# Loading the weights of experts 0 and 1 ahead of the routing, and none for empty slots

## The chip, the cores and the metric

The kernel runs on one core of a Trainium2 chip. The metric is the device time of one execution in microseconds; the time before is the median of three runs. The core has five engines that run side by side, each through its own queue of instructions in order: TensorE (PE; matmuls, with its weight loads listed as PEld), VectorE (DVE), ScalarE (ACT), GpSimd (POOL) and SyncE (SP, which here only issues transfers). Transfers between main memory and the core's own memory run on 16 DMA engines that all queues share.

## The reference

Two layers follow each other: windowed attention, and a mixture of experts in which every token goes to exactly one expert.

```python
batch, n_heads, seq, head_dim = (8, 8, 576, 64)          # q, k, v
# heads 0-3 see the last 32 positions, heads 4-7 every 4th of the last 128
scores = np.where(masks, scale * q @ k.T, -1e9)
attn = exp(scores - max) / (sum + 1e-9)
x = (attn @ v)  ->  (B*S, H*D) = (4608, 512)             # bridge

N, D, E, F = (4608, 512, 8, 1024)                        # experts
logits = x @ w_gate
expert_idx = np.argmax(logits, axis=1)
gate_w = softmax(logits)[token, expert_idx]
for e in range(E):
    h = np.maximum(x_sorted[lo:hi] @ w1[e], 0.0)         # tokens of expert e
    y_sorted[lo:hi] = h @ w2[e]
return gate_w[:, None] * y
```

The experts' weights are 8 x 4 MB in float32: w1 is 512 x 1024 and w2 is 1024 x 512 for each expert, 2 MB each.

## The kernel before

Attention goes through 32 units, four for each of the eight sequences. When a sequence is done, its tokens are routed and their rows are scattered into a table in main memory, the bucket, with one region for each expert. An expert layer is computed in *slots* of 128 tokens of one expert. There are 43 slots, since 4608 tokens and eight part-filled tiles may need that many; slots at the end may stay empty. Which expert a slot gets is only known on the chip, when enough sequences have been routed. Seven stages do this: the first (after sequence 1) settles slots 0 and 1, the next slots 2 to 5, and so on; the last, after sequence 7, settles slots 24 to 42. Slots are computed between pieces of attention as soon as they are settled, and the remaining ones after attention has ended.

Attention, unit by unit, with its loads on the SyncE queue. Each `yield` is one round, at which other work may be put between:

```python
for i in range(len(units) + LAG + 1):
    if LAG <= i < len(units) + LAG:
        eTs = weights(evs.pop(i - LAG))         # transposes of the softmax, 9 on TensorE
        yield 1.1, None
    if i < len(units):
        evs[i], dens[i] = front(qT["q"], qT["k"], units[i][1])   # scores, masks, 9 exps on ScalarE
    if 0 < i <= len(units):
        norm(evs[i - 1], dens.pop(i - 1))       # den, rec on VectorE; product on GpSimd
    yield 1.1, None
    if i > LAG:
        row_part(...)                           # transposes xrow, gate logits
        yield 0.9, b2 if (ty2, hl2) == (1, 1) else None
    if i + 1 < len(units):
        for n in "qk":
            qT[n] = turn(b2, ty2, hl2, n)       # transposes "turned"
            yield 1.0, None
        if hl2 == 1 and b2 + 1 < B:
            load_qk(b2 + 1, ty2)
    if LAG <= i < len(units) + LAG:
        for part in range(2):
            summed(eTs, b2, xT, ty2, hl2, part) # xo = softmax times v
            if part == 1 and hl2 == 1 and b2 + 1 < B:
                load_v(b2 + 1, ty2)
            yield 0.75, None
```

The tables of a stage are small VectorE operations on one partition. Their end, where it is decided whether a slot's weights differ from those two slots earlier (the weights have two buffers, for even and odd slots):

```python
exs = cpool.tile([1, NSLOT], F32, name="exs")
...
ex = exs[:, j0:j1]
nc.vector.tensor_tensor(out=ge, in0=sel, in1=experts(const("eidx", 1)), op=OP.mult)
nc.vector.tensor_reduce(out=ex, in_=ge, axis=AX, op=OP.add)     # expert of each slot
... # base: where the slot's rows begin in the bucket
new = table("new", K)
if j0 == 0:
    nc.vector.memset(new[:, 0:2], 1.0)
lo = max(j0, 2)
if lo < j1:
    nc.vector.tensor_tensor(
        out=new[:, lo - j0 : K], in0=exs[:, lo:j1], in1=exs[:, lo - 2 : j1 - 2],
        op=OP.not_equal,
    )
```

The fetches of a slot, on SyncE: its rows x, and its weights under a condition. A slot's x and w1 are fetched once the slot two before has used its w1, its w2 once that slot has used its w2. A slot without tokens carries expert 7 in the list of experts.

```python
def fetch_w(j, dst, src):
    _, n, exi, _, newi = where[j]
    rv = nc.sync.value_load(exi[:, n : n + 1], min_val=0, max_val=E - 1)
    kw = {}
    if j >= 2:
        kw["cond"] = nc.sync.value_load(newi[:, n : n + 1], min_val=0, max_val=1) > 0
    nc.sync.dma_start(
        dst[j % 2], src[ds(rv, 1)].rearrange("o (c l) f -> l (o c) f", l=128), **kw
    )

wanted = []
for j in range(NSLOT):
    wanted += [(j, "x", 0, j - 1), (j, "w1", 0, j - 1), (j, "w2", 1, j - 1)]
```

A slot's work, cut: transposes of x (`xt`, copied out by VectorE), 16 matmuls for each half of `ph` (each matmul here shows as two records), the ReLU, 8 for `py`, the scaling by the gate on ScalarE, and a scatter of the finished rows by GpSimd. From slot 36 (SURE) on each slot stands in an `If`, which is left out when the slot is empty.

```python
for j in range(NSLOT):
    if j >= SURE:
        guards.enter_context(tc.If(live[0] > j))
    ...
    xt = across(j)                               # across(j + 1) in the first half of ph
    for fg in range(2):
        ... nc.tensor.matmul(ph[:, fi], lhsT=w1[:, c, ...], rhs=xt[:, c], ...)
        if fg == 1:
            done[0] = j + 1; fetch()
    for f in range(8):
        nc.tensor.matmul(py, lhsT=h[:, f], rhs=w2[:, f], start=f == 0, stop=f == 7)
    nc.scalar.activation(y, py, AF.Copy, scale=x[:, DM : DM + 1])
    late.append(scatter)
    done[1] = j + 1; fetch()
```

How slots are put among the attention rounds: a clock in model microseconds, counted while the program is built. A stage's slots may begin `BEHIND` after its tables are done, and are spread over the time until the next stage.

```python
ATT, BEHIND = 32.0, 12.0

def run_routing():
    ...
    ahead = STAGES[n + 1][0] - b if j1 < NSLOT else 1
    ready.append((clock["all"] + BEHIND, j1, ATT * ahead + 6.0))

for cost, ended in attention():
    clock["all"] += cost
    clock["owed"] += cost * clock["rate"] / 2 + 1e-6
    run_slots()
    ...
```

The order that the engines see is made when the program is built: a scheduler may move instructions of one engine against each other where their data allow it. On SyncE it gives the transfers eight semaphores in turn.

Of the kernel before, what the change touches and what calls it, by code (L numbers as in the profile page):

```python
# [10 lines left out]
F32 = mybir.dt.float32  # L11
I32 = mybir.dt.int32
AF = mybir.ActivationFunctionType
OP = mybir.AluOpType
# [6 lines left out]
N, DM, E, F = B * S, H * DH, 8, 1024  # L21
# [9 lines left out]
NSLOT = (N + E * 127) // 128  # L31
# [63 lines left out]
def kernel(  # L95
# [10 lines left out]
    nc = tc.nc  # L106
# [22 lines left out]
    nc.vector.memset(used, 0.0)  # L129
    avail = cpool.tile([128, E1], F32, name="avail")  # L130
    nc.vector.memset(avail[:, E:E1], 4.0 * NSLOT)
    exs = cpool.tile([1, NSLOT], F32, name="exs")

    def const(name, rows=128):
        a, w = at[name]
# [225 lines left out]
    def attention():  # L361


        units = [(b, ty, hl) for b in range(B) for ty in range(2) for hl in range(2)]
        for ty in range(2):
            load_qk(0, ty)
            load_v(0, ty)
        qT = {n: turn(0, 0, 0, n) for n in "qk"}
        evs, dens, xT = {}, {}, None
        for i in range(len(units) + LAG + 1):  # L370
            if LAG <= i < len(units) + LAG:
                eTs = weights(evs.pop(i - LAG))
                yield 1.1, None
            if i < len(units):
                evs[i], dens[i] = front(qT["q"], qT["k"], units[i][1])
            if 0 < i <= len(units):
                norm(evs[i - 1], dens.pop(i - 1))
            yield 1.1, None
            if i > LAG:
                b2, ty2, hl2 = units[i - LAG - 1]  # L380
                row_part(b2, 2 * ty2 + hl2, xT)
                yield 0.9, b2 if (ty2, hl2) == (1, 1) else None
            if i + 1 < len(units):
                b2, ty2, hl2 = units[i + 1]
                qT = {}
                for n in "qk":
                    qT[n] = turn(b2, ty2, hl2, n)
# [4 lines that stand above are left out]
                b2, ty2, hl2 = units[i - LAG]  # L392
                xT = pool.tile([128, S], F32, tag="xT", name="xT", bufs=3)
                for part in range(2):
                    summed(eTs, b2, xT, ty2, hl2, part)
# [3 lines that stand above are left out]
# [125 lines left out]
    def tables(s):  # L524
# [21 lines left out]
        if last:  # L546
# [22 lines left out]
            out=upto,  # L569
# [46 lines left out]
        nc.vector.tensor_tensor(out=ge, in0=slots(place), in1=experts(begin), op=OP.is_ge)  # L616
        nc.vector.tensor_tensor(out=sel, in0=sel, in1=ge, op=OP.mult)
        yield
        ex = exs[:, j0:j1]
        nc.vector.tensor_tensor(out=ge, in0=sel, in1=experts(const("eidx", 1)), op=OP.mult)  # L620
        nc.vector.tensor_reduce(out=ex, in_=ge, axis=AX, op=OP.add)
        first, base = table("first", E1), table("base", K)
# [23 lines left out]
                out=us[:, 0:E], in0=us[:, 0:E], in1=took[:, 0:E], op=OP.add  # L646
            )
        new = table("new", K)
        if j0 == 0:
            nc.vector.memset(new[:, 0:2], 1.0)  # L650
        lo = max(j0, 2)
        if lo < j1:
            nc.vector.tensor_tensor(
                out=new[:, lo - j0 : K], in0=exs[:, lo:j1], in1=exs[:, lo - 2 : j1 - 2],
                op=OP.not_equal,
            )
        yield
        ints = []
        for name, a in (("exi", ex), ("basei", base), ("newi", new)):
            i = mpool.tile([1, K], I32, tag=f"{name}{s}", name=name, bufs=1)  # L660
# [17 lines left out]
    def fetch_w(j, dst, src):  # L678
        _, n, exi, _, newi = where[j]
        rv = nc.sync.value_load(exi[:, n : n + 1], min_val=0, max_val=E - 1)  # L680
        kw = {}
        if j >= 2:
            kw["cond"] = nc.sync.value_load(newi[:, n : n + 1], min_val=0, max_val=1) > 0
        nc.sync.dma_start(
            dst[j % 2], src[ds(rv, 1)].rearrange("o (c l) f -> l (o c) f", l=128), **kw
        )

# [109 lines left out]

    ATT, BEHIND = 32.0, 12.0  # L800

    def run_slots():

        while clock["owed"] > 0:
            while ready and ready[0][0] <= clock["all"]:
                _, upto, over = ready.pop(0)
                clock["upto"] = upto
                clock["rate"] = (SLOT * upto - clock["moe"]) / over
            if clock["moe"] >= SLOT * clock.get("upto", 0) - 0.01:
                clock["owed"] = 0.0  # L810
                return
            c = next(slots)
            clock["moe"] += c
            clock["all"] += c
            clock["owed"] -= c

    def run_routing():

        if not routing:
            return  # L820
        b, g = routing[0]
        try:
            next(g)
            clock["all"] += 0.6
        except StopIteration:
            routing.pop(0)
            fetch()
            for n, (b2, _, j1) in enumerate(STAGES):
                if b2 == b:
                    ahead = STAGES[n + 1][0] - b if j1 < NSLOT else 1  # L830
                    ready.append((clock["all"] + BEHIND, j1, ATT * ahead + 6.0))

    for cost, ended in attention():
        clock["all"] += cost
        clock["owed"] += cost * clock["rate"] / 2 + 1e-6
        run_slots()
        if ended is not None:
            routing.append((ended, route(ended)))
        run_routing()
        clock["owed"] += cost * clock["rate"] / 2  # L840
        run_slots()
# [36 lines left out]
```

## Time and profile before

| | before |
|---|---|
| median of 3 runs | 847.32 us (846.57 to 850.28) |
| span of the profiled execution | 845.4 us |
| mean granted TensorE clock | 0.969 |
| TensorE busy | 785.1 us (93%) |
| VectorE, ScalarE, GpSimd busy | 317.5, 203.3, 145.4 us |
| moved by DMA | 187.42 MB, 222 GB/s on average |
| issues of expert weights, of x rows, of output scatters | 82, 41, 39 |

In the profile's slices the span is cut into 40 equal parts of 21.1 us. A digit is the busy share of an engine in tenths, PEclk the granted TensorE clock, DMA the share of the 16 engines' time. A line of a timeline gives the start in us, the duration, the engine, the line of the kernel, the operation with what it writes and reads, how many records are merged, and in square brackets the idle time ahead of it with what ended it. A merged duration overlaps its neighbours a little, since matmuls are pipelined.

The busy times of TensorE and VectorE by stage, in us:

| stretch | length | TensorE | VectorE | DMA share |
|---|---|---|---|---|
| 0 to 120 | 120 | 88.54 | 89.33 | 0.75 |
| 120 to 160 | 40 | 35.20 | 29.16 | 1.01 |
| 160 to 200 | 40 | 39.20 | 22.69 | 0.99 |
| 200 to 250 | 50 | 47.71 | 22.23 | 0.92 |
| 250 to 550 | 300 | 297.75 | 124.18 | 0.73 |
| 550 to the end | 295.4 | 276.71 | 29.93 | 0.58 |

### The profile page before, as it was taken

The numbers are of one execution on the slowest core, as the hardware profiler recorded it, in microseconds if no ns is written. First come the engines' busy times: TensorE is split into PE (matmuls) and PEld (weight loads), VectorE is DVE, ScalarE is ACT, GpSimd is POOL, SyncE is SP. The second block draws the span as 40 slices with busy tenths as digits, with TensorE's granted clock in tenths as the row PEclk, the third lists the DMA queues.
The fourth block names the chain that finished last, engine by engine and source line by source line (L and its number), as shares of the span: only waits on it lengthen the run. The fifth ranks groups of instructions, "written<-read, shape, count | busy, mean of one in ns | idle before, by whom it ended". The sixth has DMA issues, their size and how long they took to land.

```text
span 845.4 us, 17772 instructions
## 1 busy us (share of the span) xinstructions
PE 785.1 (93%) x6830; PEld 590.7 (70%) x6830; DVE 317.5 (38%) x955; ACT 203.3 (24%) x759; POOL 145.4 (17%) x139
## 2 busy tenths in 40 slices
PE   3778779999898999999999999999999999999991
PEld 3657668776676777777777777677776768686770
DVE  3788886647332543346333631411010101111110
ACT  2564453422222222232212221110000000010100
POOL 0214332223111221103111310240000000000000
PEclk9798799999999999999999999999999999999996
DMA  9968569997999869977346566799610661659574
GB/s 202 172 130 195 128 238 314 259 257 222 322 288 322 264 224 272 281 239 259 94 169 210 194 214 235 263 378 365 213 46 25 239 216 50 221 200 338 176 266 166
DMA packets 145577, 187.42 MB, mean 222 GB/s; under 512 B 72206, under 2 KB 86030, under 8 KB 145488
## 3 DMA queue, kind: packets, MB, share of 16 engines
q1 hardware_dynamic: 137984, 165.74, 64.3%
q0 software_dynamic: 6832, 19.71, 6.6%
q8 instruction: 57, 0.93, 0.5%
q10 hardware_dynamic: 672, 0.78, 0.3%
q14 instruction: 32, 0.26, 0.1%
HBM read 216.56 MB, written 22.07 MB: 282 GB/s over the span
## 4 chain that ended last, share of the span: by engine, by line
PE 48%; issue 30%; DVE 7%; DMA 5%; ACT 3%; POOL 2%; SPq 2%; POOLq 0%; DVEq 0%; ACTq 0%
PE py L759 16%; PE ph L735 15%; PE xo L335 4%; PE weights L320 3%; DMA x<-bucket 3%; PE scores L272 3%; ACT e L295 2%; POOL out_dram L768 2%; PE xrow L414 2%; PE turned L237 1%; PE turned L245 1%; DVE lo L292 1%; PE logits L424 1%; DVE e L283 1%; DMA k<-in_k_dram 1%
## 5 line engine op out<-in xcount | busy, mean ns | idle before, releaser
L735 PE MATMUL ph<-xt,w 128*128 128x128 f32 x2496 | 304.9, 277 | 2.9 <-DVE xt L711 2.9
L735 PEld LDWEIGHTS ph<-xt,w 128*128 128x128 f32 x2496 | 292.2, 192 | 21.7 <-issue 16.9
L759 PE MATMUL py<-w,h 128*128 128x512 f32 x624 | 288.5, 600 | 0.5 <-DVE eT L322 0.5
L759 PEld LDWEIGHTS py<-w,h 128*128 128x128 f32 x624 | 110.8, 190 | 107.4 <-issue 104.1
L295 ACT ACTIVATE e<-e,lo 128x96 f32<-128x96 f32 x288 | 103.5, 362 | 78.8 <-DVE lo L292 72.6
L768 POOL DMA_INDIRECT out_dram<-y,to x39 | 38.6, 990 | 403.5 <-ACT y L763 352.5
L711 DVE COPY xt<-xt 128x512 f32<-128x512 f32 x40 | 27.5, 687 | 180.6 <-PE xt L709 180.5
L763 ACT ACTIVATE y<-py,x 128x512 f32<-128x512 f32 x39 | 26.8, 686 | 264.2 <-PE py L759 160.6
L310 POOL TENSOR_TENSOR e<-e,rec 128x864 f32<-128x864 f32 x32 | 52.1, 1629 | 205.3 <-DVE rec L309 118.1
L322 DVE COPY eT<-weights 96x384 f32<-96x384 f32 x96 | 47.8, 545 | 65.5 <-PE weights L320 65.3
L283 DVE SCALAR_TENSOR_TENSOR e<-scores,cst 128x384 f32<-128x384 f32 (+1 forms) x128 | 45.9, 397 | 42.3 <-PE scores L272 40.8
L753 DVE TENSOR_SCALAR h<-ph 128x512 f32<-128x512 f32 x39 | 26.9, 689 | 79.7 <-PE ph L735 79.7
L335 PEld LDWEIGHTS xo<-eT,v 96*64 96x64 f32 x1216 | 42.4, 144 | 18.7 <-issue 10.4
L295 ACT ACTIVATION_READ_ACCUMULATOR e<-e,lo 128x1 f32 x288 | 54.2, 188 | 0.0
L160 POOL DMA_INDIRECT bucket<-rows,idx x48 | 44.7, 932 | 37.0 <-DVE idx L513 17.5
L335 PE MATMUL xo<-eT,v 96*64 96x64 f32 (+1 forms) x1216 | 49.4, 232 | 0.0
L745 ACT ACTIVATE h<-ph 128x512 f32<-128x512 f32 x39 | 23.2, 595 | 98.7 <-PE ph L735 98.7
L320 PE MATMUL weights<-cst,e 128*96 128x128 f32 x288 | 41.4, 293 | 3.8 <-POOL e L310 3.8
L320 PEld LDWEIGHTS weights<-cst,e 128*96 128x96 f32 x288 | 34.1, 135 | 10.5 <-issue 4.9
L272 PEld LDWEIGHTS scores<-kT,qT 64*64 64x64 f32 x1152 | 31.1, 148 | 12.7 <-issue 5.8
L272 PE MATMUL scores<-kT,qT 64*64 64x96 f32 x1152 | 37.6, 268 | 2.4 <-DVE kT L242 2.3
L356 ACT COPY xT<-xo 128x288 f32<-128x288 f32 x32 | 21.1, 678 | 63.7 <-PE xo L335 63.6
(104 smaller groups left out, 459.6 us busy)
## 6 DMA issues: line engine op xcount, KB each, us to landing
w<-in_moe_w_dram SPq DMA_DIRECT2D x82, 2048.0 KB
x<-bucket SPq DMA_DIRECT2D x41, 257.0 KB
v<-in_v_dram SPq DMA_DIRECT2D x32, 192.0 KB
q<-in_q_dram SPq DMA_DIRECT2D x32, 144.0 KB
k<-in_k_dram SPq DMA_DIRECT2D x32, 144.0 KB
v<-in_v_dram SPq DMA_DIRECT2D x48, 96.0 KB
q<-in_q_dram SPq DMA_DIRECT2D x8, 576.0 KB
k<-in_k_dram SPq DMA_DIRECT2D x8, 576.0 KB
```

The source lines that it names most:

```text
L160: nc.gpsimd.indirect_dma_start(out=bucket, out_offset=bass.IndirectOffsetOnAxis(ap=idx, axis=0), in_=rows, in_offset=None, bounds_check=NR ...
L272: nc.tensor.matmul(sc[r][64 * c : 64 * c + 64, 96 * (i % 5) : 96 * (i % 5) + 96], lhsT=qT[rows, 64 * j : 64 * j + 64], rhs=kT[rows, first_ ...
L283: nc.vector.scalar_tensor_tensor(out=e[p0:p1, i : i + n].rearrange("p i k -> p (i k)"), in0=sc[r][p0:p1, cols], scalar=-SCALE, in1=const(f ...
L295: nc.scalar.activation(out=e[:, n], in_=e[:, n], func=AF.Exp, bias=lo[:, n : n + 1], scale=-1.0, accum_out=den[:, n : n + 1],)
L310: nc.gpsimd.tensor_tensor(out=e, in0=e, in1=rec.unsqueeze(2).broadcast_to([128, 9, 96]), op=OP.mult)
L320: nc.tensor.transpose(tp[0:96, 128 * i : 128 * i + 128], e[:, a + i], ident)
L322: nc.vector.tensor_copy(eT, tp[0:96, 0:384])
L335: nc.tensor.matmul(xo[DH * h : DH * h + DH, at0 : at0 + nq], lhsT=vt[:, 2 * hl + r, j, :] if ty == 0 else vt[:, hl, j, DH * r : DH * r + D ...
L711: nc.vector.tensor_copy(xt, ps)
L735: nc.tensor.matmul(ph[:, fi], lhsT=w1[:, c, 128 * f : 128 * f + 128], rhs=xt[:, c], start=c == 0, stop=c == 3,)
L759: nc.tensor.matmul(py, lhsT=h[:, f], rhs=w2[:, f], start=f == 0, stop=f == 7)
L768: i = nc.gpsimd.indirect_dma_start(out=out, out_offset=bass.IndirectOffsetOnAxis(ap=to, axis=0), in_=y, in_offset=None, bounds_check=N - 1 ...
```

## The change

The weights of experts 0 and 1 are loaded without condition into the two buffers during sequence 1, before any routing is known. The list of experts gets two entries in front, 0 and 1, so that slots 0 and 1 are compared with what the buffers already hold, as every other slot is compared with the slot two before. In the last stage the condition is also multiplied by "this slot has tokens", so that no weights are fetched for an empty slot. Since the first weights may now already be there, slots 0 and 1 may begin 4 instead of 12 model microseconds behind their tables. It is meant to take the first weight loads out of the wait between the first routing and the first slot, and to spare loads that nobody uses.

```diff
-    exs = cpool.tile([1, NSLOT], F32, name="exs")
+    exs = cpool.tile([1, 2 + NSLOT], F32, name="exs")
+    for i in range(2):
+        nc.vector.memset(exs[:, i : i + 1], float(i))
...
-        ex = exs[:, j0:j1]
+        ex = exs[:, j0 + 2 : j1 + 2]
...
-        if j0 == 0:
-            nc.vector.memset(new[:, 0:2], 1.0)
-        lo = max(j0, 2)
-        if lo < j1:
-            nc.vector.tensor_tensor(
-                out=new[:, lo - j0 : K], in0=exs[:, lo:j1], in1=exs[:, lo - 2 : j1 - 2],
-                op=OP.not_equal,
-            )
+        nc.vector.tensor_tensor(
+            out=new, in0=exs[:, j0 + 2 : j1 + 2], in1=exs[:, j0:j1], op=OP.not_equal
+        )
         yield
+        if last:
+            nc.vector.scalar_tensor_tensor(
+                out=new, in0=sel[:, :, E], scalar=0.5, in1=new, op0=OP.is_lt, op1=OP.mult
+            )
...
     def fetch_w(j, dst, src):
-        kw = {}
-        if j >= 2:
-            kw["cond"] = nc.sync.value_load(newi[:, n : n + 1], min_val=0, max_val=1) > 0
+        new = nc.sync.value_load(newi[:, n : n + 1], min_val=0, max_val=1)
         nc.sync.dma_start(
-            dst[j % 2], src[ds(rv, 1)].rearrange("o (c l) f -> l (o c) f", l=128), **kw
-        )
+            dst[j % 2], src[ds(rv, 1)].rearrange("o (c l) f -> l (o c) f", l=128), cond=new > 0
+        )
+
+    def load_first(j):
+        for dst, src in ((w1s, moe_w1), (w2s, moe_w2)):
+            nc.sync.dma_start(dst[j], src[j].rearrange("(c l) f -> l c f", l=128))
...
+    FIRST = 30
...
-                    ready.append((clock["all"] + BEHIND, j1, ATT * ahead + 6.0))
+                    behind = BEHIND if n else 4.0
+                    ready.append((clock["all"] + behind, j1, ATT * ahead + 6.0))
+
+    rounds = 0
     for cost, ended in attention():
+        rounds += 1
+        if rounds in (FIRST, FIRST + 6):
+            load_first(int(rounds > FIRST))
         clock["all"] += cost
```

Round 30 falls into the second unit of sequence 1, round 36 into the third.

More of the change, by code (lines that the diff above doesn't have):

```diff
@@ L648, in tables @@
         new = table("new", K)
-        if j0 == 0:
-            nc.vector.memset(new[:, 0:2], 1.0)
-        lo = max(j0, 2)
-        if lo < j1:
-            nc.vector.tensor_tensor(
-                out=new[:, lo - j0 : K], in0=exs[:, lo:j1], in1=exs[:, lo - 2 : j1 - 2],
-                op=OP.not_equal,
+        nc.vector.tensor_tensor(
+            out=new, in0=exs[:, j0 + 2 : j1 + 2], in1=exs[:, j0:j1], op=OP.not_equal
+        )
+        yield
+        if last:
+            nc.vector.scalar_tensor_tensor(
+                out=new, in0=sel[:, :, E], scalar=0.5, in1=new, op0=OP.is_lt, op1=OP.mult
             )
-        yield
         ints = []
```

## The prediction

> **What bounds the kernel now.** I read the summary page first: engine shares, then the slices.
>
> ```profile
> PE 785.1 (93%) x6830; PEld 590.7 (70%) x6830; DVE 317.5 (38%) x955; ACT 203.3 (24%) x759; POOL 145.4 (17%) x139
> ...
> PE   3778779999898999999999999999999999999991
> ...
> DVE  3788886647332543346333631411010101111110
> ...
> PEclk9798799999999999999999999999999999999996
> DMA  9968569997999869977346566799610661659574
> ```
>
> TensorE is busy 785.1 of 845.4 us, so 60.3 us is all that scheduling can win back, plus what the clock loses. In the windows 31.5 us of that idle lies before 120 us, where only attention runs and VectorE is busy 74%. Another 18.7 us lies after the last matmul, which ends near 826.7. Between 120 and 826.7 about 10 us is left. The change acts around 50 to 160 us and on the prefetches that follow, so I listed TensorE's idle pieces there from the timeline and kept those of 0.4 us and more.
>
> ```profile
> 118.16 0.53 PE L424 MATMUL logits<-xT,wg 128*32 128x192 f32 x6 [0.78 <-ACT xT L356]
> ...
> 126.77 1.26 PE L735 MATMUL ph<-xt,w 128*128 128x128 f32 x8 [2.95 <-DVE xt L711]
> ...
> 129.17 2.06 PE L735 MATMUL ph<-xt,w 128*128 128x128 f32 x8
> ...
> 137.63 0.37 PE L440 MATMUL lg<-cst,lgs 96*96 96x96 f32 x2 [1.35 <-DVE lgs L437]
> ...
> 148.21 1.12 PE L759 MATMUL py<-w,h 128*128 128x512 f32 x2 [0.48 <-DVE eT L322]
> ...
> 199.09 0.37 PE L494 MATMUL rank<-before,cst 96*96 96x48 f32 x2 [0.80 <-DVE before L481]
> ...
> 218.21 0.63 PE L709 MATMUL xt<-cst,x 128*128 128x128 f32 x4 [2.29 <-DMA x<-bucket]
> ...
> 262.13 0.63 PE L709 MATMUL xt<-cst,x 128*128 128x128 f32 x4 [2.25 <-DMA x<-bucket]
> ```
>
> No piece names a weight load. Slot 0's first expert matmul (126.77) waits for VectorE's copy of xt; the trace's landing record puts slot 0's w1, issued at 114.97, in SBUF at 123.6, three microseconds earlier. VectorE's timeline says why the copy is late: it stands behind other work in its queue.
>
> ```profile
> 121.25 0.17 DVE L307 TENSOR_SCALAR den<-den 128x9 f32<-128x9 f32 x1 [0.57 <-ACT e L295]
> ...
> 126.03 0.68 DVE L711 COPY xt<-xt 128x512 f32<-128x512 f32 x1
> ```
>
> The two late x rows have another cause. In SyncE's timeline each is issued late and behind bulky transfers:
>
> ```profile
> 205.02 0.40 SPq L684 DMA_DIRECT2D w<-in_moe_w_dram  x1
> 206.26 0.37 SPq L676 DMA_DIRECT2D x<-bucket  x1
> ...
> 247.21 6.93 SPq L188 DMA_DIRECT2D q<-in_q_dram  x4
> 254.24 3.32 SPq L188 DMA_DIRECT2D k<-in_k_dram  x4
> 258.93 0.37 SPq L676 DMA_DIRECT2D x<-bucket  x1
> ```
>
> The x issued at 206.26 sits behind 2 MB of weights from 205.02 and is used at 218.21. The x of 258.93 could not be issued until q and k had been, whose issue was stretched to 10 us.
>
> **What the Trainium skill says.** "DMA: Bandwidth & Descriptors", section "Queues, rings and completion order": within one queue the descriptors are consumed in ring order. The trace agrees: an x of 257 KB needs 2.5 us on a quiet queue (issued 113.76, landed 116.25) and about 11 us behind the weights of 205.02. The same page, "Why small descriptors are slow (HBM only)": short runs carry a fixed cost each. Here the packet records show 184 to 203 GB/s while 256-byte runs of q, k and v fill the engines (80 to 85 us, 140 to 145 us) and 399 GB/s for weights (120 to 135 us), with the 16 engines full in both. "TensorE: Matmul & The Clock Gate", section "Part 1: The HAM clock gate (the "warmup" mystery)": an idle window of about 3.4 us halves the matmul clock. The trace has a half-clock stretch from 127.7 to 131.1, just after the 2.95 us hole; in it eight matmuls take 2.06 us (129.17), against 1.06 at 132.06, a loss of some 1.7 us.
>
> **The change, part by part.**
>
> *Which experts are fetched.* Running the routing on the reference's inputs gives slot 0 expert 0 and slot 1 expert 2, since after two sequences expert 1 has only 119 tokens and no full tile. So slot 0's fetch is dropped, the early load of expert 1 is wasted, and slot 1 still fetches. Slots 39 to 42 are empty: 39 tiles are live, as the 39 scatters show. Before, fetches go out for 29 of the 41 slots reached (82 issues, 24 of them skipped, by the trace); after, for 26. In transfers of 2.1 MB: 58 before, 26*2 + 4 = 56 after. That is 4.2 MB less of 187.4, and no time by itself.
>
> *The early load.* In the built program w1 and w2 of expert 0 stand behind q and k of sequence 2, issued 44.6 to 49.4, and those of expert 1 behind the v rows of sequence 1 (54.0 to 61.4). At 399 GB/s 8.4 MB is 21 us of full engines. Between 50 and 100 us the packets occupy 29.5 of 50 us, so it just fits. The program's order also shows that each SyncE transfer waits for the one eight before it. So from the 7th on, the v pieces of 54.0 wait for expert 0, until about 51.5 + 10.5 = 62; they land near 68 and are read at 79.25, no loss. Then expert 1 takes 68 to about 82, with the 1.2 MB of row scatters that run from 65 to 77. The q and k issued at 61.5 and 62.4 now land near 85 to 87 and are read at 85.77 and 86.33: a loss of 0 to 1.5 us, I take 0.7. What follows has room again (v issued 73.65, read 98.6).
>
> *Slot 0 earlier.* The delay before the first slots falls from 12 to 4 model microseconds. In TensorE's order slot 0's transposes move up from behind the turn of 121.91 to between the q and k turns of 114.89 and 115.44. With x landed near 116 they end at 116.7, the k turn at 117.3. But VectorE's copy of xt now stands behind a den that needs nine exponentials. ACT has them ahead of its two xT copies now, so they start after lo (116.4) and take 3.1 us as before; den, rec, to and xt then end near 120.8. So the hole is again about 3.6 us, with the clock likely halved again (1.7 us). The holes of 0.60 to 2.95 us between 113 and 127 are thus exchanged for one of like size. Check: up to the lg transposes of sequence 3, the new order holds four more ph groups (4.4 us), one xt (0.6) and three py (2.7) than the old, so equal holes put lg's end of 138.0 at 145.7; adding durations along the new order gives about 145. Gain here about 0.5. The lgs wait of 1.35 now has two py matmuls ahead of it: gain about 1.
>
> *Prefetches afterwards.* Slot 1's weights alone follow stage 0, 4.2 MB less in the queue: 10.5 us less backlog at 140. Slots 0 and 1 also end about 10 us earlier. The order of SyncE changes with it: w1 and w2 of slot 3 now stand ahead of the v pieces of sequence 4 instead of around them, so slot 4's x no longer follows a just issued w2; and slot 6's x stands ahead of q and k of sequence 6 instead of behind. Both waits, 2.29 + 2.25 = 4.5 us, should go. I keep 1.5 us back for a new wait of this kind, as w2 of slot 6 now stands behind those q and k: gain 3.
>
> *The rest.* VectorE gains two tiny memsets and one op of 19 elements in the last table, about 0.15 us each like its neighbours; two extra register loads on SyncE for each of the first four fetches delay slot 1's weights by about 1 us, and they are needed 25 us later.
>
> *The tail.* The last w2 of before is for an empty slot and lands at 836.7. But GpSimd's records after its last scatter (827.76) show four semaphore increments of about 2.04 us each, one per empty slot, and from 836.7 a drain of 7.8 us, which ends the program. None of this is a weight load, and from slot 20 on TensorE runs without holes. I count 0.
>
> Sum: -0.7 + 0.5 + 1 + 3 = 3.8 us gained: 847.3 - 3.8 = 843.5.
>
> **Rivals.**
> 1. *The copy of xt takes the whole gain*, or slot 0 ahead of attention matmuls delays the softmax chain, and later x rows wait anew. For it: the VectorE queue above, and DMA slices at 9 up to 400 us. Against: after 127 TensorE always has slot work to fill in. It gives 846 to 850.
> 2. *The early load collides with attention*: q and k late by 3 to 5 us, nothing hidden behind, as attention alone runs then. For it: the engines would be full from 51 to 95. Against: the reads are 11 to 24 us behind the issues. It gives 847 to 851.
> 3. *The tail shortens*: the drain at the end waits for SyncE's last weight load, both being at 836.7. For it: that coincidence. Against: the four increments reach 836.67 by themselves. It gives 838 to 840.
>
> **Range and chances.** I put about 55% on the main course, 30% on the first two rivals, 15% on the third. Range 838.5 to 848.5. Two per cent is 17 us, more than all holes from 107 to 826.7 together (about 12 us plus the clock), so faster 0.015; slower by 17 us would need repeated starvation, 0.015; same 0.97.
>
> **What would show it.** Right: slot 0's transposes near 116 with a hole of 3 to 4 us behind them before the first ph; no wait for x near 200 to 265; half clock near 120; q and k read at about 86 with at most 1.5 us of idle. Wrong: weight or x waits over 1 us after 145, a last matmul after 826, or an end closer than 18 us behind the last matmul, which would mean the tail did depend on the empty slots' weights.

## The result and the profile after

The changed kernel takes **860.25 us** (median of 4 runs, 858.79 to 861.24), the kernel before 848.8 us beside it (4 runs, 846.57 to 852.03). The ratio is **1.0131**, 95% interval 1.0090 to 1.0171. It is slower by about 11 us; the prediction had 843.5, range 838.5 to 848.5. The profiled execution spans 858.0 us (before 845.4) at a mean granted clock of 0.954 (before 0.969).

The summary page of the changed kernel, the lines that answer to those shown of before:

```profile
PE 797.1 (93%) x6830; PEld 600.9 (70%) x6830; DVE 316.4 (37%) x958; ACT 204.7 (24%) x759; POOL 145.7 (17%) x139
...
PE   3877788989999999999999999999999999999991
...
DVE  3787584844743363336333541231101010101010
...
PEclk9788678989999999999999999999999999999996
DMA  9898958789799868979336557799710571659500
```

TensorE's idle time is what it was: 858.0 - 797.1 = 60.9 us, before 60.3. Its *busy* time grew by 12.0 us, although it runs the same 6830 matmul records. The slices say how: in the fourth to eighth (64 to 172 us) PEclk reads 8, 6, 7, 8, 9, before 8, 7, 9, 9, 9; and DMA, which was at 6, 8, 5 in the third to fifth before, reads 9, 8, 9 there.

To place the loss I cut both spans at two marks of TensorE's timeline: the `lg` transposes that begin the routing of sequence 0 and of sequence 1 (60.31 and 94.99 before, 61.95 and 107.46 after), and the last `py` (826.1 and 838.8). Windows of the kernel before; the columns are start and end, length, then busy time and records of TensorE, its weight loads, VectorE, ScalarE and GpSimd, then granted clock, DMA share, GB/s:

```profile
60.31:94.99 34.68, 27.73 (x443) 22.42 (x443) 28.69 (x79) 18.71 (x87) 10.95 (x11) 0.88 0.66 156
94.99:826.10 731.11, 718.34 (x5794) 536.16 (x5795) 248.83 (x771) 157.21 (x552) 123.00 (x116) 0.99 0.71 231
```

The same windows of the changed kernel:

```profile
61.95:107.46 45.51, 35.23 (x443) 28.57 (x443) 29.52 (x79) 18.88 (x86) 12.50 (x11) 0.73 0.94 238
107.46:838.80 731.34, 721.74 (x5795) 539.70 (x5795) 246.76 (x774) 158.42 (x552) 121.76 (x115) 0.98 0.67 218
```

Of the 12.6 us between the two spans 10.8 (45.51 - 34.68) lie between the marks, that is in sequence 1, where the early load was put. The 1.6 us ahead of the first mark are no part of it: in the repeat of the changed kernel (e13 below) this mark stands at 60.20. What follows takes as long as before (731.34 against 731.11), and from the last `py` to the end it is 19.3 us in both. In sequence 1 the idle time grew by 3.3 us (6.95 to 10.28), the busy time of the same 443 matmuls by 7.5 us. The clock record has 24.2 us at half clock in this stretch, before 8.3; the 15.9 us more, at half speed, are up to 8 us of lost work, enough for that growth. **I call this stretch, lg to lg, the sequence-1 stretch; it is the measure of the experiments.**

TensorE's idle pieces of 1 us and more from 80 us on, and the one that names k, in the changed kernel's timeline:

```profile
85.60 1.26 PE L323 MATMUL weights<-cst,e 128*96 128x128 f32 x9 [3.48 <-POOL e L313]
...
92.97 1.15 PE L417 MATMUL xrow<-cst,xT 128*96 128x128 f32 x6 [2.41 <-ACT xT L359]
...
96.69 1.19 PE L248 MATMUL turned<-cst,k 72*128 72x72 f32 x8 [0.63 <-DMA k<-in_k_dram]
...
107.46 0.55 PE L443 MATMUL lg<-cst,lgs 96*96 96x96 f32 x2 [2.30 <-DVE lgs L440]
...
127.93 0.63 PE L715 MATMUL xt<-cst,x 128*128 128x128 f32 x4 [1.02 <-DMA x<-bucket]
...
132.88 2.07 PE L741 MATMUL ph<-xt,w 128*128 128x128 f32 x8 [3.83 <-DVE xt L717]
...
184.22 0.47 PE L240 MATMUL turned<-cst,k 96*128 96x96 f32 x3 [3.07 <-DVE xt L717]
```

Only one piece names a transfer of attention (k, 0.63 us). The two largest in sequence 1 name GpSimd's product `e` and ScalarE's copy of `xT`. In the kernel before, the same two places had 0.66 and 1.10 us:

```profile
81.27 1.19 PE L320 MATMUL weights<-cst,e 128*96 128x128 f32 x9 [0.66 <-POOL e L310]
...
84.53 0.86 PE L414 MATMUL xrow<-cst,xT 128*96 128x128 f32 x6 [1.10 <-ACT xT L356]
```

Two other queues show what became late. SyncE's timeline before, between 54 and 65 us:

```profile
54.02 7.40 SPq L216 DMA_DIRECT2D v<-in_v_dram  x13
61.53 0.35 SPq L191 DMA_DIRECT2D q<-in_q_dram  x1
62.41 0.31 SPq L191 DMA_DIRECT2D k<-in_k_dram  x1
```

and after:

```profile
50.51 2.36 SPq L692 DMA_DIRECT2D w<-in_moe_w_dram  x2
55.71 14.56 SPq L219 DMA_DIRECT2D v<-in_v_dram  x13
70.72 0.94 SPq L692 DMA_DIRECT2D w<-in_moe_w_dram  x2
71.77 6.96 SPq L194 DMA_DIRECT2D q<-in_q_dram  x1
78.82 2.37 SPq L194 DMA_DIRECT2D k<-in_k_dram  x1
...
83.46 13.45 SPq L206 DMA_DIRECT2D v<-in_v_dram  x4
```

The v pieces took 14.56 us to issue, since the eighth waits until 67.56 for expert 0's weights. Expert 1's load follows, and q is only issued *behind both*: at 71.77 instead of 61.53, and its issue alone lasts 6.96 us. By the landing records w2 of expert 1 is there at 90.08, q at 93.61 and k at 96.56. SyncE never catches up inside sequence 1: the next q starts at 97.00, before at 78.86.

GpSimd's timeline before, and then after, at the first work behind sequence 0's row scatters:

```profile
77.82 0.24 POOL L408 TENSOR_SCALAR rows<-cst 96x6 f32<-96x6 f32 x1 [3.66 <-PE xrow L414]
79.58 1.63 POOL L310 TENSOR_TENSOR e<-e,rec 128x864 f32<-128x864 f32 x1 [1.53 <-DVE rec L309]
```

```profile
83.59 0.24 POOL L411 TENSOR_SCALAR rows<-cst 96x6 f32<-96x6 f32 x1 [7.72 <-DMA bucket<-rows,idx]
83.91 1.63 POOL L313 TENSOR_TENSOR e<-e,rec 128x864 f32<-128x864 f32 x1
```

The small initialisation of a new `rows` tile waits until the last scatter that reads the old one has landed (by the landing record 83.41, before 77.63), and the softmax product `e` stands behind it in GpSimd's order. So TensorE's weights transposes start at 85.60.

### The profile page after: what moved, and what is told of

It is laid out like the page before. It is cut to its first block, busy times and chain, and to the rows that moved or that the text cites. A ratio compares the mean times of both kernels' runs of the same rounds, so it can differ in the third digit from the quotient of the medians.

```text
span 858.0 us, 17796 instructions
## 1 busy us (share of the span) xinstructions
PE 797.1 (93%) x6830; PEld 600.9 (70%) x6830; DVE 316.4 (37%) x958; ACT 204.7 (24%) x759; POOL 145.7 (17%) x139
## 2 busy tenths in 40 slices
DMA packets 144009, 183.23 MB, mean 214 GB/s; under 512 B 72174, under 2 KB 85998, under 8 KB 143920
## 4 chain that ended last, share of the span: by engine, by line
PE 54%; issue 29%; DMA 5%; DVE 5%; POOL 2%; ACT 2%; SPq 1%; POOLq 0%; ACTq 0%; DVEq 0%
PE ph L741 18%; PE py L765 16%; PE xo L338 5%; PE weights L323 4%; PE scores L275 3%; DMA k<-in_k_dram 3%; PE xrow L417 2%; ACT e L298 2%; POOL out_dram L774 2%; DMA x<-bucket 2%; PE turned L248 1%; PE logits L427 1%; PE turned L240 1%; PE xt L715 1%; DVE e L286 1%
## 5 line engine op out<-in xcount | busy, mean ns | idle before, releaser
L741 PEld LDWEIGHTS ph<-xt,w 128*128 128x128 f32 x2496 | 293.8, 193 | 22.7 <-issue 15.9
L298 ACT ACTIVATE e<-e,lo 128x96 f32<-128x96 f32 x288 | 103.6, 361 | 94.1 <-DVE lo L295 91.7
L717 DVE COPY xt<-xt 128x512 f32<-128x512 f32 x40 | 27.6, 689 | 192.4 <-PE xt L715 192.3
L338 PEld LDWEIGHTS xo<-eT,v 96*64 96x64 f32 x1216 | 45.3, 151 | 18.4 <-issue 10.7
L338 PE MATMUL xo<-eT,v 96*64 96x64 f32 (+1 forms) x1216 | 52.8, 240 | 0.1
L163 POOL DMA_INDIRECT bucket<-rows,idx x48 | 44.8, 934 | 32.4 <-DVE idx L516 17.1
L323 PEld LDWEIGHTS weights<-cst,e 128*96 128x96 f32 x288 | 35.6, 139 | 12.6 <-POOL e L313 7.0
```

What stands on the lines that cost most here:

```text
L163: nc.gpsimd.indirect_dma_start(out=bucket, out_offset=bass.IndirectOffsetOnAxis(ap=idx, axis=0), in_=rows, in_offset=None, bounds_check=NR ...
L298: nc.scalar.activation(out=e[:, n], in_=e[:, n], func=AF.Exp, bias=lo[:, n : n + 1], scale=-1.0, accum_out=den[:, n : n + 1],)
L323: nc.tensor.transpose(tp[0:96, 128 * i : 128 * i + 128], e[:, a + i], ident)
L338: nc.tensor.matmul(xo[DH * h : DH * h + DH, at0 : at0 + nq], lhsT=vt[:, 2 * hl + r, j, :] if ty == 0 else vt[:, hl, j, DH * r : DH * r + D ...
L717: nc.vector.tensor_copy(xt, ps)
L741: nc.tensor.matmul(ph[:, fi], lhsT=w1[:, c, 128 * f : 128 * f + 128], rhs=xt[:, c], start=c == 0, stop=c == 3,)
```

## The experiments

Theory A: the bytes of the early load collide with what attention needs (the prediction's second rival, but larger). Theory B: the load's instructions alone make the scheduler order attention's instructions worse; the built programs show that TensorE then takes the next nine weights transposes and 18 scores matmuls ahead of 18 of the 20 `xo` matmuls of one unit (the first of the second head type in sequence 1), and ScalarE takes the exponentials that come next ahead of that unit's xT copies. Theory C: the earlier start of slots 0 and 1 costs time by itself.

Runs e9 to e12 and e17, e18 fell on chips on which the kernel before itself takes 886 us, with further TensorE idle: pieces of up to 1 us that are named issue, and 3 to 4 us for ScalarE's copy of `rows` (3.54 us at 76.47 in e12). Their ratios are against that time, and their stretches are set only beside each other. Every stretch comes from one profiled execution; the changed kernel's own two are 45.5 and 47.4 us.

### e1 to e4: parts of the change, one at a time

e1 keeps the early loads as instructions but under a condition that never holds, so no bytes move (and the list of experts says that the buffers hold nothing). e2 has no early load at all. e3 loads expert 0 only. e4 lets the first slots begin at 12 again.

```diff
 # e1
-            nc.sync.dma_start(dst[j], src[j].rearrange("(c l) f -> l c f", l=128))
+            nc.sync.dma_start(dst[j], src[j].rearrange("(c l) f -> l c f", l=128), cond=no > 0)
 # e2: both lines left out; e3: load_first(0) at FIRST only
-        if rounds in (FIRST, FIRST + 6):
-            load_first(int(rounds > FIRST))
 # e1, e2: exs starts with -1, -1; e3: with 0, -1
-        nc.vector.memset(exs[:, i : i + 1], float(i))
+        nc.vector.memset(exs[:, i : i + 1], (-1.0, -1.0)[i])
 # e4
-                    behind = BEHIND if n else 4.0
+                    behind = BEHIND
```

> The changed kernel with its four early transfers under a condition that is always false, and slots 0 and 1 fetching their own weights: the instruction order of the changed kernel on every engine, but no early bytes. Theory A (the early bytes collide with the attention stage: the row scatter of sequence 0 lands at 83.4 instead of 77.6, GpSimd's next row initialisation waits for it and holds back the softmax product e): the loss goes, 845 to 851 us, and the first slot's x is issued near 114 as before. Theory B (the build order made with the early loads, which puts weights and scores ahead of most of the xo matmuls, is what delays the stage): the loss stays, 856 to 862, x issued near 122 or later. Theory C (slots 0 and 1 starting earlier cost the time): also 856 to 862, but with x issued near 114.

> The changed kernel without the early loads at all; slots 0 and 1 fetch their weights after the routing, slots still start 4 model microseconds behind their tables, empty slots are skipped. A and B: 845 to 851. C: 855 to 862. If A and B are both wrong, as C.

> The changed kernel with the early load of expert 0 alone; slot 1 fetches as before. Theory A: the row scatter no longer shares the engines with expert 1's 4 MB, so GpSimd goes on near 79 and the loss is mostly gone: 847 to 852. Theory B: the order in which xo stands behind scores comes from expert 0's load and is still there, so the loss stays above 855.

> The changed kernel with the first slots 12 instead of 4 model microseconds behind their tables. Theory A and B: the loss is made before 113 us and stays, 857 to 863. Theory C: 846 to 851.

| | median us | ratio, interval | stretch us |
|---|---|---|---|
| before (44 runs here; stretch of the first pair) | 850.72 | 1 | 34.7 |
| e1 order, no bytes | 857.69 | 1.0092, 1.0067 to 1.0116 | 41.8 |
| e2 no early load | 852.47 | 1.0013, 0.9988 to 1.0038 | 34.6 |
| e3 expert 0 only | 857.45 | 1.0084, 1.0048 to 1.0119 | 44.8 |
| e4 slots at 12 | 857.64 | 1.0108, 1.0022 to 1.0195 | 45.8 |

e2 clears everything but the early load, in time and in the stretch, though slot 0 then waits 5.91 us for its weights (125.23). e1 seemed to say that seven of the eleven microseconds were Theory B, without a byte moved. That reading was too simple, as e13 to e15 show; its x is issued at 118.92, between what the theories wanted. e3 comes out as Theory B wanted it (above 855), but GpSimd waits for the scatter there too (7.16 us), so it doesn't part the two theories. e4 keeps the loss: the earlier slots are not its main cause.

### e5, e6: the load behind q and k

The loads are placed in rounds 44 and 48, behind q and k of sequence 2; the order of attention up to slot 0 is then nearly that of before. e5 has the slots at 12, e6 at 4.

```diff
-    FIRST = 30
+    FIRST = 44
-        if rounds in (FIRST, FIRST + 6):
+        if rounds in (FIRST, FIRST + 4):
```

> The change with the early load placed 14 rounds later (rounds 44 and 48, behind the transfers of v of sequence 1 and of q and k of sequence 2) and the first slots again 12 model microseconds behind their tables. The order of TensorE's attention instructions up to slot 0 is then that of before but for a few. If the order of instructions carries most of the loss: the stretch between the lg transposes of sequences 0 and 1 comes back to 34.5 to 36.5 us (before 34.7, changed kernel 45.5), and the time is 843 to 849. If the bytes carry it: the stretch is 38 us or more and the time 850 to 854.

> The same late load, but with the first slots 4 model microseconds behind their tables, as in the change. If the earlier slots cost time of their own (new hole behind the copy of xt, half clock after it): 3 to 6 us above the run with 12, in the time from the lg transposes of sequence 1 to the last py too (726 against 731 in the two runs with the early load in the change's place). If not: within 1.5 us of it.

e5: 854.01 us, ratio 1.0032 (1.0003 to 1.0060), stretch 40.0. e6: 858.92, ratio 1.0074 (1.0047 to 1.0101), stretch 38.0. By e5's own expectation the bytes win: in the stretch they cost less than in the change's place, but 3 to 5 us. The victims moved along. In e5 GpSimd again stands 8.18 us for the row scatter (83.61), TensorE 3.55 us behind it (85.62), and now the *next* q is stretched to 12.35 us behind expert 1's load (issued 89.56). Between e5 and e6 the medians differ by 4.9 us, as Theory C says, with intervals that just overlap; the two traces don't show it (773.2 and 772.1 us from the first `lg` to the last `py`).

### e7, e12: GpSimd's wait for the scatter

The token numbers of the `rows` tile are written by VectorE in the routing, so GpSimd has nothing to wait for. e7 does so in the changed kernel, e12 in the kernel before.

```diff
-            nc.gpsimd.tensor_scalar(rows[b][:, :, DM + 1], const("tok", TT), float(b * S), None, op0=OP.add)
...
         nc.vector.reciprocal(row[:, :, DM], gate)
+        nc.vector.scalar_tensor_tensor(out=row[:, :, DM + 1], in0=gate, scalar=0.0,
+            in1=const("tok", TT)[:, b * NT : b * NT + NT], op0=OP.is_ge, op1=OP.mult)
```

> The changed kernel, but the column of token numbers is written by VectorE in the routing instead of by GpSimd when the rows tile is begun, so GpSimd no longer stands and waits for sequence 0's row scatter (idle of 7.72 us before its operation at 83.59). If the late landing of that scatter is what the early load's bytes do to sequence 1: no TensorE idle behind GpSimd's e near 85 (3.48 there), the stretch between the two lg transposes 41.5 to 43 us instead of 45.5, time 856 to 858. If the bytes act elsewhere (q, k, v landing late): the stretch stays within 1 us and the time is 859 to 861.

> The kernel before with the token numbers written by VectorE instead of GpSimd, nothing else. GpSimd's wait for the row scatter costs before only 0.66 us of TensorE in sequence 1 and later sequences have slot work to fill in: ratio 0.997 to 1.001. A ratio below 0.995 would say that this wait costs more than its one hole.

e7: 860.18 us, ratio 1.0098 (1.0067 to 1.0129), stretch 44.9. The hole behind `e` fell from 3.48 to 1.57 us, and nothing was won: TensorE now waits 1.81 us for q (94.13), 1.93 us for k (97.25) and 3.03 us for xT (90.01). GpSimd's wait is only the first of several that stand side by side. e12: ratio 1.0000 (0.9974 to 1.0026).

### e8: the empty slots alone

The kernel before, with only the condition in the last stage.

```diff
         yield
+        if last:
+            nc.vector.scalar_tensor_tensor(
+                out=new, in0=sel[:, :, E], scalar=0.5, in1=new, op0=OP.is_lt, op1=OP.mult
+            )
```

> The kernel before with one part of the change alone: no weights fetched for slots without tokens. Prediction's step for the tail, worth 0: ratio 0.997 to 1.003, and the end 18.5 to 19.5 us behind the last py. If the end had waited for the last useless weight load: 3 to 8 us faster.

850.53 us, ratio 0.9997 (0.9975 to 1.0020), the end 19.3 us behind the last `py`. This part moves 8.4 MB less (179.03 against 187.42 MB) and costs and gains nothing.

### e9 to e11 and e13 to e16: the order kept, with and without the bytes

An ordering without a semaphore keeps attention as before: the weights transposes of the next unit stay behind the last `xo` matmul of the unit named above, and, for the two units of that head type, the exponentials that come next stay behind the unit's first xT copy. The loads stay where the change has them. Up to slot 0 TensorE and ScalarE then have the order of before, but for the order within one group of `xo` matmuls.

```diff
+    def behind(late, early):
+        tc.add_manual_dep(ins(late), ins(early).name, mybir.DependencyInfo(
+            mybir.DependencyClass.NoSync, mybir.DependencyReason.DATA), reason="order")
...
                 eTs = weights(evs.pop(i - LAG))
+                if i > LAG and units[i - LAG - 1] == (1, 1, 0):
+                    behind(held["weights"], held["xo"])
...
                     summed(eTs, b2, xT, ty2, hl2, part)
+                    if (b2, ty2) == (1, 1) and part == 0:
+                        for n in range(9):
+                            behind(held["exp", n], held["xT", 0])
```

e9 and e14 are the change with this order; e10 and e15 also move no bytes (as e1); e16 is e14 with the slots at 12; e11 is e16 with e7's edit; e13 is the changed kernel again.

> The changed kernel with the early load in its place, but with the order of before kept in sequence 1: by added ordering the nine weights transposes of the next unit stay behind the xo matmuls of the unit whose v was late in the model, and the exponentials stay behind the first xT copy of the units of that head type. If the order carries most of the loss: the stretch between the lg transposes of sequences 0 and 1 is 37.5 to 40.5 us (before 34.7, changed kernel 45.5) and the time 851 to 856. If the order had only followed the bytes, so that TensorE now waits for v, q and k instead: 43 us or more, and 858 to 862.

> Control to the run that kept the order of the change without its transfers (857.69 us, ratio 1.0092, stretch 41.8 us): the same kernel, no early transfers, with the order of before kept in sequence 1. If the order alone cost that: stretch 34.5 to 36 us, and the time of the run without any early load, ratio 0.999 to 1.004. If it was something else that the skipped transfers leave behind on SyncE: stretch above 40 us, ratio above 1.007.

> The early load in its place, the order of before kept, the token numbers written by VectorE so that GpSimd does not wait for the row scatter, and the first slots 12 model microseconds behind their tables. If order, GpSimd's wait and the earlier slots are all that the loss is made of: stretch 35 to 37.5 us and ratio 0.998 to 1.003. If the bytes delay q, k and v by themselves: stretch 38 us or more and ratio 1.004 to 1.008.

| chip with before at 886.11 | median us | ratio, interval | stretch us |
|---|---|---|---|
| e9 order kept, bytes | 902.86 | 1.0176, 1.0138 to 1.0213 | 43.8 |
| e10 order kept, no bytes | 897.93 | 1.0140, 1.0106 to 1.0174 | 40.0 |
| e11 order kept, bytes, e7's edit, slots at 12 | 893.04 | 1.0064, 1.0031 to 1.0098 | 48.0 |
| e12 before with e7's edit | 884.88 | 1.0000, 0.9974 to 1.0026 | 40.3 |

The stretches are as Theory B wants them without bytes (e10 as e12) and as Theory A wants them with bytes: 3.8 us more in e9, 7.7 in e11, where GpSimd doesn't wait and TensorE stands 2.58 us for q (95.02) and 1.80 us for k (98.02). The ratios follow another line. From the `lg` of sequence 1 to the last `py`, e9 takes 773.0, e10 772.7 us with the slots at 4, e11 762.0 and e12 759.6 with the slots at 12 (e17 and e18 on a like chip: 769.8 and 766.2). That is as Theory C wants it, by 4 to 13 us, but it is not shown by these pairs: e11 and e12 also have e7's edit, e12 has no early load, and e18 has its load in another place. 6.08 us of e10 are a wait for slot 0's weights.

> The changed kernel itself once more, beside the three that follow, since the four runs just before were on a chip on which the kernel before takes 886 us and TensorE shows idle that is named issue. Here both theories expect a ratio of 1.009 to 1.017 if the kernel before takes 847 to 852 us, and a stretch from lg to lg of 44 to 47 us.

> The change with its traffic and the order of before kept in sequence 1, as in e9. Order: stretch 37.5 to 40.5 us and a ratio 0.4 to 0.9 per cent under that of the change beside it. Bytes alone: stretch 43 us or more, ratio within 0.3 per cent of the change's.

> As e10: no early transfers, order of before. Order: stretch 34.5 to 36.5 us, ratio 0.999 to 1.004, against 1.0092 and 41.8 us with the order of the change. If SyncE's skipped transfers were the cause: stretch above 40 us and ratio above 1.007.

> The change with its traffic, the order of before kept, and the first slots 12 model microseconds behind their tables. If the earlier slots cost by themselves, as they seem to with the late load (1.0032 with 12, 1.0074 with 4): 0.3 to 0.6 per cent under e14. If not: within 0.2 per cent of e14.

| chip with before at 847.74 | median us | ratio, interval | stretch us |
|---|---|---|---|
| e13 changed kernel | 860.48 | 1.0150, 1.0114 to 1.0187 | 47.4 |
| e14 order kept, bytes | 859.64 | 1.0160, 1.0101 to 1.0219 | 47.5 |
| e15 order kept, no bytes | 854.77 | 1.0082, 1.0034 to 1.0130 | 35.8 |
| e16 order kept, bytes, slots at 12 | 858.25 | 1.0113, 1.0071 to 1.0156 | 45.2 |

e14 overturns the reading of e1: **with the bytes there, the order is worth nothing** (47.5 against 47.4 us, ratios 1.0160 and 1.0150). Its timeline, TensorE:

```profile
84.69 2.16 PE L324 MATMUL weights<-cst,e 128*96 128x128 f32 x9 [4.13 <-POOL e L314]
...
94.65 1.19 PE L249 MATMUL turned<-cst,q 72*128 72x72 f32 x8 [4.13 <-DMA q<-in_q_dram]
97.08 1.19 PE L249 MATMUL turned<-cst,k 72*128 72x72 f32 x8 [1.24 <-DMA k<-in_k_dram]
```

GpSimd's wait is as in the change. The xT wait of 92.97 is gone, and where TensorE comes earlier it meets q, which has not landed (landing records: w2 of expert 1 at 91.22, q at 94.51, k at 96.94): 4.13 + 1.24 us. In the changed kernel the bad order filled just that time, and so hid the late q behind names that are no transfer. The same place in e15, without the bytes:

```profile
83.21 1.19 PE L324 MATMUL weights<-cst,e 128*96 128x128 f32 x9 [0.61 <-POOL e L314]
...
86.92 0.86 PE L432 MATMUL xrow<-cst,xT 128*96 128x128 f32 x6 [1.55 <-ACT xT L368]
```

So in the stretch there are two causes, and they don't add: the bytes with the order of before lengthen it from 35.8 to 47.5 us, which is the whole loss, the order without bytes from 35.8 to 41.8 (e15 and e1, on different chips), about half of it, and both together come to 45.5 and 47.4.

The total does not follow the stretch. e1 and e15 can't be told apart (1.0092 and 1.0082, some 7 us each), though their stretches differ by 6 us; and e15 should have come out as e2 (1.0013). What e15 loses is not settled: its first `ph` waits 6.22 us for slot 0's weights (125.86), but so does e2's, 5.91 us.

Nor is Theory C settled on this kind of chip. e5 against e6 favours the later slots by 0.4%. e16 against e14 does so by 0.5% in the ratios, but by 0.16% in the medians, since one of e14's four runs took 867.79 us; by the expectation's own limit that is no difference. Behind the stretch the traces have 729.7 us in e14 and 731.5 in e16, but with the change's order 726.2 in e4 against 731.3 and 730.1 in the changed kernel and its repeat.

### e17, e18: one expert only

e17 is e14 with expert 0 alone, so that no weights stand directly ahead of q. e18 loads expert 0 alone, in e5's place, with the slots at 12.

```diff
-        if rounds in (FIRST, FIRST + 6):
-            load_first(int(rounds > FIRST))
+        if rounds == FIRST:
+            load_first(0)
```

> As e14 (order of before kept, slots 4 behind), but only expert 0 is loaded early, in the change's place: 4.2 MB instead of 8.4 MB in sequence 1, and no bulk transfer stands directly ahead of q and k of sequence 2 on SyncE. If q and k are late because expert 1's descriptors stand ahead of them in the same queue: q's issue takes under 1 us instead of 7.4, TensorE waits under 1.5 us for q and k together instead of 5.4, the stretch is 38 to 41 us instead of 47.5. If expert 0's load does it alone, since the v pieces wait for it and q stands behind them: the stretch is 43 us or more.

> The version with the least that can collide: only expert 0, issued behind q and k of sequence 2, where SyncE has 11 us without an issue, slots 12 behind their tables, empty slots not fetched. If the queue position and the bytes are all: stretch 35 to 38 us and ratio 0.997 to 1.003. If any load in sequence 1 costs several us: stretch above 39 us and ratio above 1.004.

Before takes 885.68 us here. e17: 897.13 us, ratio 1.0117 (1.0050 to 1.0184), stretch 40.9. e18: 889.26, ratio 1.0034 (1.0011 to 1.0058), stretch 39.6. On the like chip of e9 to e12 the stretch was 40.3 (e12) and 40.0 (e10) without bytes, 43.8 (e9) with both experts. SyncE's timeline of e17:

```profile
57.87 15.12 SPq L220 DMA_DIRECT2D v<-in_v_dram  x13
73.52 0.31 SPq L195 DMA_DIRECT2D q<-in_q_dram  x1
```

The v pieces are as slow as in the change, so q is issued as late. But it goes out in 0.31 us instead of 6.96, TensorE waits for neither q nor k (last landing records 81.52 and 85.62; e14 has 94.51 and 96.94), and the stretch is within a microsecond of that without any load. So the late q is the work of expert 1's 4 MB ahead of it in its own queue. The time does not follow here either: e17 stays 1.2% above before. And GpSimd's wait is still there on this chip (7.23 us before the `rows` initialisation at 85.24) and only hidden, since `e` waits for VectorE's `rec` until 89.58. In e3, on the other kind of chip, it cost 3.47 us with expert 0 alone. So the scatters are late without expert 1's weights too; and since q goes out in 0.31 us there as well (69.65) and no wait names it, e3's stretch of 44.8 us, with the order of the change, doesn't need the late q.

e18's stretch shows no loss, but from the `lg` of sequence 1 to that of sequence 2 it takes 50.3 us, e12 45.3. SyncE's next v issue takes 7.23 us there instead of 2.27, the q behind it goes out 2.2 us later, but no wait of TensorE names them. TensorE is busy 4.6 us longer with the same 480 records (40.41 against 35.85) at a granted clock of 0.73 against 0.85; what brings the half clock there is open. The early load is not free in this place either. No version faster than the kernel before was found; the skipped fetches (e8) can be kept for their 8.4 MB.

## Why the prediction was wrong

**The step that failed** is the early load: "Then expert 1 takes 68 to about 82", and from it "The q and k issued at 61.5 and 62.4 now land near 85 to 87 and are read at 85.77 and 86.33: a loss of 0 to 1.5 us, I take 0.7." Its term of the sum, 0.7 us, measures 10.8 us in the profiled pair, nearly the whole of the 11.5 us between the medians; without the early load (e2) the ratio is 1.0013. Three things in it were wrong.

1. *How long the loads take.* The place in the queue was right: the prediction has q and k land behind expert 1's weights, in ring order, as the Trainium skill says in "DMA: Bandwidth & Descriptors", section "Queues, rings and completion order", and the landings agree (w2 at 90.08, q at 93.61, k at 96.56). But expert 0 was given 10.5 us and took 17.0 (50.51 to 67.54), expert 1 was given 14 and took 19.4 (70.72 to 90.08). 399 GB/s had been reckoned for the weights; in these two stretches the full engines (shares 1.06 and 0.99) moved 306 and 307 GB/s of everything together. So q and k came 8 to 10 us later than predicted. With no weights ahead of it (e17) the issue of q took 0.31 us instead of 6.96.
2. *The row scatters were only counted as a load on the weights.* They were delayed themselves: from the first issue to the last landing 14.8 us (68.62 to 83.41), before 10.7 (66.92 to 77.63). And GpSimd, in order, held the softmax product behind them: 3.48 us of TensorE, 2.8 more than before. The same section says that a DMA engine takes turns between its queues packet by packet, and the later landings are in line with it. The other packets need not be weights: with expert 0 alone, which had landed before the first scatter was issued, the scatters took 14.2 (e3) and 14.3 us (e17). In e3 the packets of q and k, pushed back behind expert 0, ran beside them until 80.9; in the kernel before they were through near 70.
3. *"So it just fits" was a sum of free engine time between 50 and 100 us.* It did not hold. The engines moved 140 GB/s at a share of 0.59 there before, 269 GB/s at 0.97 after: 7.0 MB and the 8.4 MB of weights would be 15.4 MB, and 13.4 MB went through. Some 2 MB were pushed past 100 us.

The half clock then cost more than the holes: 3.3 us more idle, 7.5 us more busy time. I had charged it for one hole (1.7 us).

Open stays how the total splits. The stretch is the work of bytes and order, as e13 to e15 show; but e1 and e15 move no early byte and still lose 7 us, and in e15 the stretch is as long as before.

**The second rival** named the right cause and was sized too small: "q and k late by 3 to 5 us, nothing hidden behind", 847 to 851. In e14 the waits for q and k are 5.4 us, close to what it said; GpSimd's wait and the clock were missing in it.

**Slot 0 earlier** (+0.5): the mechanism was right. The copy of xt stands behind `den`, whose exponentials come late, as VectorE's timeline of the changed kernel shows:

```profile
131.79 0.17 DVE L310 TENSOR_SCALAR den<-den 128x9 f32<-128x9 f32 x1 [2.66 <-ACT e L298]
...
132.15 0.68 DVE L717 COPY xt<-xt 128x512 f32<-128x512 f32 x1
```

The hole is 3.83 us (predicted 3.6), the clock halves behind it (131.0 to 137.8). But the transposes start at 127.93, not near 116, since the stretch ahead of them is longer. The sign of the term is not settled by the pairs with 4 and 12.

**The lgs wait** (+1): gone as predicted. **Prefetches** (+3): both x waits of 2.29 and 2.25 us are gone, and no weight wait came. A wait for slot 1's xt copy did (3.07 us at 184.22), again with half clock behind it (185.6 to 192.4). Behind the stretch idle fell by 3.2 us (12.77 to 9.60) and busy time rose by 3.4, so of the predicted 4.5 us nothing is left.

**The tail** (0): right, by e8 and by the 19.3 us from the last `py` to the end. The third rival falls. **The count of transfers** was right: 183.23 MB against 187.42.

Of the signs named, "a last matmul after 826" came true as wrong (838.8), "no wait for x near 200 to 265" as right; "at most 1.5 us of idle" at q and k came true for k (0.63 us) and was no sign at all, since the bad order stood in front of it.

## What to carry to other kernels

A transfer that nobody waits for yet still has a place in an in-order queue: before moving it, list what stands behind it there and work out *its* landing again, at the rate that full engines gave to everything together and not at the rate of the bulk transfer alone; then see who else waits in order behind the transfers of that time. When a run without the bytes shows a loss, do not book the rest to the bytes: take away the first cause with the bytes in place as well, for each may hide the other. Where TensorE has no other work to fill in, a hole costs more than itself, for the half clock after it: here 3.3 us more of holes came with 7.5 us more of busy time.

## What the runs showed of the hardware

- The half-clock stretches ahead of the tail last 3.4, 6.8, 10.2 or 13.7 us, in every run. That fits the free-running window of about 3.4 us of the Trainium skill, "TensorE: Matmul & The Clock Gate", section "Part 1: The HAM clock gate (the "warmup" mystery)". But in this kernel they also follow holes shorter than the window: after 2.41 us (92.97) the clock is half from 93.4 to 103.6. In the changed kernel they sum to 64.9 us before the tail, against 37.5 before.
- The issue of one q transfer of SyncE took 0.35 us in a free queue, 6.96 and 8.22 us behind 4 MB of weights (changed kernel and its repeat; 3.09 to 7.36 in the other runs with both loads in this place), and one of four later v pieces 7.24 us.
- The same program took 848 to 851 us on three chips and 886 us on two others, with TensorE idle that is named issue or ScalarE's copy of `rows`. One kernel came out at 1.0140 on one kind (e10) and 1.0082 on the other (e15), with intervals that just overlap: an effect of a few us is compared on one chip only.
